# Sums of weight blocks: begun from SBUF, with GpSimd's queue doing the copies and additions in HBM

## The chip, the cores and the metric

The kernel runs on one core of a Trainium2 chip. Its time is the device time of one execution in microseconds (us). Before the change three runs took 359.33, 360.73 and 356.85 us, a median of 359.33. The profiled execution is one more run, of 360.87 us.

The engines are named as in the profile: PE multiplies matrices, PEld loads its weights, DVE is the vector engine, ACT the scalar engine, POOL is GpSimd, and SP only issues transfers. Each engine works through its own list of instructions in order. If one waits, everything behind it on that engine waits too. Transfers (DMAs) are issued here from SP's queue, and those that add to what is already at their destination from GpSimd's queue.

## The reference

Linear attention with product features, and behind it a block with a spatial gate. For every one of 4 batches:

```python
# attention, per head: phi(x) = outer product of S1 x and S2 x, flattened
kv  = einsum('bhsf,bhsd->bhfd', k_p, v);  z = sum(k_p, axis=2)
out = einsum('bhsf,bhfd->bhsd', q_p, kv) / (einsum('bhsf,bhf->bhs', q_p, z) + 1e-6)
# block: x is out with its heads side by side, (4, 1088, 128)
h = gelu(x @ w_in)                      # 1088 x 1024
u, v = h[..., :512], h[..., 512:]
v_n = (v - mean) / sqrt(var + 1e-6) * g_ln
v_s = einsum('ts,bsd->btd', w_sg, v_n) + b_sg    # the large product, 1088 x 1088
result = x + (u * v_s) @ w_out
```

The large product with `w_sg` is most of PE's work.

## The kernel before

All numbers are float32. A matrix is cut into a high and a low part (`w_h`, `w_l`, each of a form that PE multiplies fast), and a product takes three matmuls: high by high, low by high, high by low. `w_sg` transposed lies in SBUF as nine tiles of 128 rows by 1088 columns. The raw tiles are `w_f[0]` to `w_f[8]`. The pool that they lie in has ten buffers, so `w_l[0]` takes the tenth and `w_l[t]` the buffer of `w_f[t-1]` (`w_lo`, L806). `w_h` is cast on ACT (L798). The 1088 columns are cut in three (`CH`: 362, 362, 364).

From batch 1 on the kernel does not multiply with the first eight tiles and first two column blocks as they are. These make four quarters, and a scheme of the Strassen family (`pair`) uses seven products in place of eight. It needs four sums of quarters. `sums` makes them in HBM as `ud["1"]` to `ud["4"]`, each of 128 x 4 x 362 numbers (724 KB):

- `ud1` is the first four tiles' columns 0 plus their columns 1 (blocks of 362),
- `ud3` is columns 1 of the first four tiles plus columns 1 of the next four,
- `ud2` is `ud1` plus columns 1 of the next four,
- `ud4` is `ud2` plus columns 0 of the next four.

Before the change each sum begins with a copy within HBM on SP's queue (L1034), from the input or from an earlier sum, and then a DMA on GpSimd's queue adds the other quarter from the input to it (L1035).

`combine` brings each sum back in 16 steps (a sum's quarter of 181 KB each): a load into one of two `tmp` buffers (L1044), a cast to the high part on ACT (L1050), a subtraction for the low part on DVE (L1051), and two stores to `td` in HBM (L1052, L1053). The last four steps go straight to the tile `t4` in SBUF (L1046, L1047). It also stores the present block's parts (`td<-w_h` in one DMA, L1038, and `td<-w_l`, L1040). `stream` loads a sum's parts from `td` over a block of `w_h` and `w_l` just before the product that uses it (L1058, L1060).

`attention(b)` does the next batch's attention beside this batch's product. For each of three column pieces it loads q (`qld`, L1102), casts it on ACT (L1103), multiplies, stores the result to `dq` (L1114), and loads it back spread over partitions as `ea` (L1124) and `eb` (L1121). DVE multiplies these (L1127). Nine times it makes features of k: a small ACT copy `kb` (L1080), a DVE product `kp` (L335), two matmuls (L1085).

Batch 0 starts with a head (`Head`), whose order is a list of times (`HEAD`). What follows is ordered by `Plan`: every step is added with its engine, an assumed duration, what it reads and writes by key, and how long after its end others can use it (`late`). `order` then goes greedily: among the engines' next candidates it takes the step that can begin soonest, and among equals the one whose latest start is soonest. Each engine's clock begins at `START`. PE's own order comes from positions (`SIDE`, `UNITS`, `OUTS`). A key that no planned step has written counts as there from time 0: the planner does not know of the head's casts to `w_h`, so for it `td<-w_h` has no dependency. The planner decides only the order; on the chip real waits hold each engine.

The subtractions `w_l[t]` (L806, 1.29 in the planner) are steps of the plan. PE's low-half products of batch 0 (L1396) need them; the high-half ones (L1398, L1400) need only `w_h`. The subtraction for tile 8 also issues a memset on GpSimd (L805).

Of the kernel before, what the change touches and what calls it, by code (L numbers as in the profile page):

```python
# [9 lines left out]
F32 = mybir.dt.float32  # L10
# [4 lines left out]
ALU = mybir.AluOpType  # L15
# [19 lines left out]
START = dict(PE=51.0, V=50.5, A=49.5, G=42.0, SP=22.0)  # L35
# [3 lines left out]
        k=[-5.4506e+25, -1.86798e+26, -3.68831e+26, 1.20378e+26, -7.9147e+25, -9.67116e+25, 1.96766e+26, -2.06105e+26, 6.74955e+26],  # L39
        m=[7.0166e+17, 2.77359e+17, -3.64635e+17, 8.10316e+17, 1.97376e+17, -8.45712e+17, -4.46692e+17, -1.41243e+17, -1.88428e+17],  # L40
        q=[-9.85222e+37, 5.31737e+37, 4.53485e+37],
        n=[-274.09, -244.17, 66.1, 49.89, 93.41, 9.07],
        v=[76.03, 83.8, 72.28, 135.63, 69.13, 141.32, 90.81, 19.91, 17.47],
    ),
    dict(
        k=[593.03, 652.39, 759.38, 737.29, 443.29, 501.8, 757.29, 665.05, 583.46],
        m=[181.66, 55.3, 177.71, 207.99, 164.59, 28.04, 351.09, 71.24, 278.52],
        q=[311.71, 57.77, 475.27],
        n=[37.39, 79.03, 123.68, 46.32, 129, 236.43],
        v=[580.02, 111.55, 375.1, 240.14, 317.92, 200.21, 237.14, 270.19, 333.5],  # L50
    ),
    dict(
        k=[422.85, 473.07, 417.68, 478.31, 460.36, 386.01, 441.63, 346.1, 261.67],
        m=[301.77, 360.33, 343.21, 360.38, 350.42, 350.94, 332.88, 347.33, 369.39],
        q=[1146.3, 742.29, 1592.44],
        n=[984.53, 1257.57, 989.65, 894.74, 1102.64, 2169.93],
        v=[167.65, 154.05, 141.48, 171.91, 152.85, 155.69, 151.39, 163.95, 152.38],
# [3 lines left out]
    [-1.04603e+28, 1.31879e+27, 9.14156e+27],  # L61
    [3.41858e+18, 2.84867e+18, -6.26725e+18],
    [-189.15, -288.19, -100.37],
    [-50.81, 43.38, -20.02],
    [109.48, -67.17, 142.22],
    [148.1, -7.29, 2.09],
    [1056.04, 327.23, 85.89],
    [95.05, -21.61, 86.97],
    [117.32, 22.47, 794.73],
    [80.72, 480.77, 387.65],  # L70
    [-70.9, 427.98, 208.86],
    [-72.96, 32.18, 19.81],
    [1076.4, 485.65, 90.51],
    [2270, 600.47, 693.56],
    [395.39, -72.81, 275.88],
    [540.79, -121.68, 468.41],
]
OUTS = [
    [7.95, 65.22, 185.79],
    [-235.12, 49.59, -10.2],  # L80
    [30.85, -17.35, 3.84],
    [29.71, 41.29, 67.24],
    [211.45, -1.34, -11.66],
    [2.71, 252.59, 31.55],
    [237.53, 4.98, 393.45],
    [-7.96, 76.75, 88.15],
    [196.45, 360.61, 338.7],
    [19.67, 0.34, -44.95],
    [694.41, 120.49, 438.77],
    [26.72, 571.51, 1075.44],  # L90
    [202.88, 487.56, 87.11],
    [125.31, -0.94, 517.67],
    [304.16, 133.75, 3.31],
    [2.8, 474.19, 4.5],
# [161 lines left out]
def tile_kernel(ctx: ExitStack, tc: tile.TileContext, qd, kd, vd, sd, wd, bd, wind, gd, woutd, identd, outd):  # L256
    nc = tc.nc
    mm = nc.tensor.matmul
    V, A, G = nc.vector, nc.scalar, nc.gpsimd
    load = nc.sync.dma_start  # L260
# [41 lines left out]
    w_f, w_l = {}, {}  # L302
# [29 lines left out]
    def features(out, a, b):  # L332

        sh = [P, 2, R, 2, R]
        V.tensor_tensor(  # L335
            out.rearrange("t (p i h j) -> t p i h j", p=2, i=R, h=2),
            a[:, :32].rearrange("t (p i h) -> t p i h", p=2, i=R).unsqueeze(4).broadcast_to(sh),
            b.rearrange("t (p h j) -> t p h j", p=2, h=2).unsqueeze(2).broadcast_to(sh),
            op=ALU.mult,
        )  # L340
# [121 lines left out]
    class Head:  # L462
# [7 lines left out]
        def load(self, name, ns, f, after=()):  # L470
            self.s.at(name, "SP", 0.47, f, after, late=-ns)
# [377 lines left out]
    def load_(_, kb, f, **kw):  # L849
        return add("SP", 0.47, f, kb=kb, **kw)  # L850
# [10 lines left out]
    def ps(k):  # L861
        return pst[plan.got[k]]
# [20 lines left out]
    for t in range(NT):  # L883
        lo = add("V", 1.29, head.s.steps["wlo", t][2], w=[("w", t, c, 1) for c in range(3)], after=[lo] if t else [])
    done_lo = lo
# [138 lines left out]
    K2 = HW * 2  # L1024
# [3 lines left out]
    ud = {n: dram.tile([P, 4, K2], F32, name=f"ud{n}") for n in "1324"}  # L1028

    def sums():  # L1030
        part = lambda i, j: wd[:, 4 * i : 4 * i + 4, K2 * j : K2 * j + K2]
        for n, first, more in (("1", part(0, 0), part(0, 1)), ("2", "1", part(1, 1)), ("3", part(0, 1), part(1, 1)), ("4", "2", part(1, 0))):
            u = isinstance(first, str)
            load_("", 741, lambda n=n, f=first, u=u: load(ud[n], ud[f] if u else f), r=[("ud", first)] * u, w=[("ud", n)])  # L1034
            add("G", 1.2, lambda n=n, m=more: G.dma_start(ud[n], m, accum_op=ALU.add), w=[("ud", n)], late=7.0)  # L1035

    def combine():
# [25 lines left out]
    def attention(b):  # L1063
# [9 lines left out]
        for t in range(NT):  # L1073
# [7 lines left out]
            add("V", 0.38, lambda t=t, pk=pk: features(kpt[t % 3], ps(pk)[:, :P], kbt[t % 2]), r=[pk, ("kb", t % 2)], w=[("kp", t % 3)], free=[pk])  # L1081
# [297 lines left out]
    sums()  # L1379

# [95 lines left out]
```

## Time and profile before

| | |
|---|---|
| median of three runs | 359.33 us |
| profiled execution | 360.87 us |
| its span, first to last instruction | 359.1 us |
| mean granted TensorE clock | 0.976 |
| HBM read, written | 49.10 MB, 14.93 MB |
| DMA bytes on SP's queue, on GpSimd's | 55.05 MB, 2.97 MB |

In the timelines a row is: start and duration in us, engine, line, operation, what it writes and reads (buffer numbers left out), how many, and in brackets the idle time of the engine before it with what ended that. In a chain row there is only the start, the duration and the step; a chain's DMA row runs from issue to landing. In the rows of time stretches a pair is busy us and number of instructions for PE, PEld, DVE, ACT and POOL, and then come the granted clock of PE (1.00 is full), the mean busy share of the 16 DMA engines and GB/s. A DMA queue's row has packets, MB and the time of its packets as a share of 16 engines' time in the stretch. A row with "<-" and three numbers behind a colon is a wait: us in all, times, longest.

### The profile page before, as it was taken

Reading aid. Unit: us, or ns where it says so; the run is one execution under the profiler, and the core shown is the slowest. Engines: PE = TensorE matmul, PEld = TensorE weight load, DVE = VectorE, ACT = ScalarE, POOL = GpSimd, SP = SyncE. Lnnn points to the kernel's source line nnn. Section 1 sums busy time; section 2 is a strip of 40 time slices with the busy share of each in tenths; the row PEclk is TensorE's granted clock in tenths of the full one; section 3 lists DMA queues with packets and bytes.
Section 4 is the critical chain, followed back from the end, with each engine's and each line's share of the span. In section 5 each row is a group of like instructions: output and inputs, shape, how many; then the busy total and the mean of one; then the engine's idle time right before and its main releaser. Section 6 shows DMA issues by size and latency. Waiting matters only on the chain.

```text
span 359.1 us, 5751 instructions
## 1 busy us (share of the span) xinstructions
PE 338.1 (94%) x1952; PEld 316.2 (88%) x1952; DVE 260.0 (72%) x573; ACT 214.1 (60%) x509; POOL 28.4 (8%) x90
## 2 busy tenths in 40 slices
PE   8999999697499979999999999999999999999995
PEld 7867669696497979999999999998999999999994
DVE  4798999683766556989972688976885696674753
ACT  5476871360469977745679975657869552333421
POOL 0004001110000220000003300000041200000000
PEclk9999999899599998999999999999999999999999
DMA  7999997989357763595038506650005437002631
GB/s 251 394 374 299 174 228 166 236 271 204 114 150 241 219 195 92 164 340 157 21 102 259 150 15 191 185 192 4 2 0 168 165 112 242 0 23 60 181 112 62
DMA packets 41965, 58.47 MB, mean 163 GB/s; under 512 B 4080, under 2 KB 39216, under 8 KB 41904
## 3 DMA queue, kind: packets, MB, share of 16 engines
q1 hardware_dynamic: 39680, 55.05, 48.9%
q0 software_dynamic: 2112, 2.97, 6.2%
q8 instruction: 15, 0.25, 0.3%
q14 instruction: 14, 0.11, 0.1%
q10 hardware_dynamic: 144, 0.09, 0.1%
HBM read 49.10 MB, written 14.93 MB: 178 GB/s over the span
## 4 chain that ended last, share of the span: by engine, by line
PE 58%; DMA 16%; ACT 10%; DVE 8%; SPq 2%; issue 2%; POOL 1%; POOLq 0%; DVEq 0%; ACTq 0%
PE bz L992 10%; PE bz L994 10%; PE bz L993 10%; DMA eb<-dq 8%; DMA tmp<-ud 3%; DMA td<-tmp 3%; PE pz L792 3%; ACT vn L407 2%; PE pab L668 2%; ACT kp L1182 2%; DMA dq<-ab 2%; PE bs L1085 2%; ACT vn L1179 2%; PE bs L906 2%; PE bs L908 1%
## 5 line engine op out<-in xcount | busy, mean ns | idle before, releaser
L992 PE MATMUL bz<-w_h,ar 128*128 128x362 f32 (+1 forms) x288 | 97.3, 338 | 0.7 <-ACT ar L967 0.3
L994 PE MATMUL bz<-w_l,ar 128*128 128x362 f32 (+1 forms) x288 | 95.4, 331 | 0.0
L993 PE MATMUL bz<-w_h,ar 128*128 128x362 f32 (+1 forms) x288 | 95.4, 331 | 0.0
L992 PEld LDWEIGHTS bz<-w_h,ar 128*128 128x128 f32 x288 | 55.0, 191 | 2.9 <-DVE gt L922 1.7
L993 PEld LDWEIGHTS bz<-w_h,ar 128*128 128x128 f32 x288 | 55.0, 191 | 0.5
L994 PEld LDWEIGHTS bz<-w_l,ar 128*128 128x128 f32 x288 | 55.0, 191 | 0.0
L912 ACT ACTIVATE u<-bs 128x362 f32<-128x362 f32 (+1 forms) x48 | 22.6, 472 | 20.1 <-PE bs L908 13.6
L936 ACT CAST gh<-gt 128x362 fp32r<-128x362 f32 (+1 forms) x47 | 23.1, 493 | 16.7 <-DVE gt L935 9.7
L967 ACT CAST ar<-vn 128x512 fp32r<-128x512 f32 x37 | 22.8, 618 | 16.9 <-PE bz L994 15.9
L407 ACT ACTIVATE vn<-vn,st 128x512 f32<-128x512 f32 x36 | 27.5, 809 | 6.6 <-POOL st L538 2.6
L937 DVE TENSOR_TENSOR gl<-gt,gh 128x362 fp32r<-128x362 f32 (+1 forms) x47 | 24.8, 531 | 9.0 <-ACT gh L936 8.9
L935 DVE TENSOR_TENSOR gt<-gt,u 128x362 f32<-128x362 f32 (+1 forms) x47 | 24.8, 530 | 6.5 <-ACT u L912 6.1
L922 DVE SCALAR_TENSOR_TENSOR gt<-bz,g_col,b_bc 128x362 f32<-128x362 f32 (+1 forms) x37 | 21.9, 592 | 10.3 <-PE bz L1004 8.0
L968 DVE TENSOR_TENSOR ar<-vn,ar 128x512 fp32r<-128x512 f32 x37 | 25.3, 686 | 5.6 <-ACT ar L967 5.4
L906 PE MATMUL bs<-x_h,win_h 128*128 128x362 f32 (+1 forms) x48 | 17.0, 355 | 7.4 <-ACT u L912 7.4
L1127 DVE TENSOR_TENSOR ea<-ea,eb 128x728 f32<-128x728 f32 (+1 forms) x9 | 8.2, 914 | 20.2 <-DMA eb<-dq 20.2
L1182 ACT ACTIVATE kp<-vn,st 128x512 bf16<-128x512 f32 x27 | 19.4, 719 | 0.2
L1179 ACT ACTIVATE vn<-bs 128x512 f32<-128x512 f32 x27 | 16.0, 593 | 5.7 <-PE bs L1172 5.6
L1085 PE MATMUL bs<-vx,kp 128*128 128x128 f32 x108 | 16.5, 277 | 2.0 <-DVE kp L335 2.0
L792 PE MATMUL pz<-w_f,vn 128*128 128x362 f32 (+3 forms) x54 | 17.6, 472 | 0.5 <-ACT vn L407 0.5
L1085 PEld LDWEIGHTS bs<-vx,kp 128*128 128x128 f32 x108 | 14.8, 192 | 2.6 <-DVE kp L335 2.5
L906 PEld LDWEIGHTS bs<-x_h,win_h 128*128 128x128 f32 x48 | 9.4, 196 | 8.2 <-ACT u L912 7.7
(267 smaller groups left out, 757.0 us busy)
## 6 DMA issues: line engine op xcount, KB each, us to landing
w_l<-td SPq DMA_DIRECT2D x52, 181.0 KB
w_h<-td SPq DMA_DIRECT2D x26, 362.0 KB
w_f<-in_w SPq DMA_DIRECT2D x9, 544.0 KB
td<-tmp SPq DMA_DIRECT2D x24, 181.0 KB
ud<-in_w POOLq DMA_DIRECT2D x4, 724.0 KB, 11.5
tmp<-ud SPq DMA_DIRECT2D x16, 181.0 KB
vx<-in_v SPq DMA_DIRECT2D x8, 288.0 KB
ea<-dq SPq DMA_DIRECT2D x12, 182.0 KB
```

The source lines that it names most:

```text
L407: A.activation(self.vn(t), self.vn(t), AF.Identity, bias=self.nm[:, t : t + 1], scale=self.rs[:, t : t + 1])
L792: return mm(zs[ci], lhsT=vn[r, t, :P], rhs=w_f[t][r, c0 : c0 + cw], start=(t == 0), stop=(t == NT - 1),)
L906: mm(o, lhsT=win_h[:, ws], rhs=xh[:, cs], start=True, stop=False)
L935: add("V", dv(cw), lambda: V.tensor_mul(gt(k)[:, :cw], gt(k)[:, :cw], utt[plan.got[u]][:, :cw]), r=[u], w=[k], free=[u])
L937: add("V", dv(cw), lambda: V.tensor_sub(glt[plan.got[l]][:, :cw], gt(k)[:, :cw], f32(ght[plan.got[h]][:, :cw])), r=[h, k], take={l: "gl"}, ...
L968: add("V", dv(n), lambda: V.tensor_sub(dst[:, 1], q(), f32(dst[:, 0])), r=r, w=[key])
L992: mm(o, lhsT=ar[e][:, 0, t], rhs=wh, start=first, stop=False, skip_group_check=True)
L993: mm(o, lhsT=ar[e][:, 1, t], rhs=wh, start=False, stop=False, skip_group_check=True)
L994: mm(o, lhsT=ar[e][:, 0, t], rhs=wl, start=False, stop=last, skip_group_check=True)
L1085: mm(ps(pkv)[:, P * p : P * p + P], lhsT=kpt[t % 3][:, P * p : P * p + P], rhs=vx[:, NT : NT + t + 2 : t + 1] if p else vx[:, t : NT + 1 : ...
L1179: A.activation(g.vn(t), pair(ps(pv)), AF.Gelu_apprx_tanh, accum_out=g.mv[:, t, 0:1])
L1182: A.activation(pair(waste), g.vn(t), AF.Square, bias=g.mv[:, t, 0:1], scale=1.0, accum_out=g.mv[:, t, 1:2])
```

## The change

- `ud` is laid out as 4 tiles of 128 x 362, each tile in one piece.
- `ud1` and `ud3` begin with four stores each from the raw tiles in SBUF, on SP's queue, and four additions each from SBUF, on GpSimd's queue, 181 KB apiece.
- `ud2` and `ud4` begin with a copy within HBM that is now on GpSimd's queue, followed by the addition from the input as before.
- The raw tiles are now read by these transfers, so `w_l[t]` has to wait for the readers of `w_f[t-1]`. The steps for `w_l` are added to the plan behind `sums`, and the plan is told of this by the key `wf`; it assumes that the raw tiles are there at 31.0.
- `combine` takes the sums in the order 1, 3, 2, 4.
- The planner's numbers change: an addition of 181 KB is there 6 us after its issue, a copy 11, an addition of 724 KB 12 (7 before); `w_l` takes 1.2, `kp` 0.335; the clocks of GpSimd and SP begin at 34 and 24. The positions in `SIDE`, `UNITS` and `OUTS` are all new numbers.

```diff
-START = dict(PE=51.0, V=50.5, A=49.5, G=42.0, SP=22.0)
+START = dict(PE=51.0, V=50.5, A=49.5, G=34.0, SP=24.0)
...
     for t in range(NT):
-        lo = add("V", 1.29, head.s.steps["wlo", t][2], w=[("w", t, c, 1) for c in range(3)], after=[lo] if t else [])
-    done_lo = lo
+        add(None, 0, None, w=[("wf", t)], start=31.0)
...
-    ud = {n: dram.tile([P, 4, K2], F32, name=f"ud{n}") for n in "1324"}
+    ud = {n: dram.tile([4, P, K2], F32, name=f"ud{n}") for n in "1324"}
+
+    def plus(out, x, **kw):
+        add("G", 1.1, lambda: G.dma_start(out(), x, accum_op=ALU.add), late=6.0, **kw)
 
     def sums():
-        part = lambda i, j: wd[:, 4 * i : 4 * i + 4, K2 * j : K2 * j + K2]
-        for n, first, more in (("1", part(0, 0), part(0, 1)), ("2", "1", part(1, 1)), ("3", part(0, 1), part(1, 1)), ("4", "2", part(1, 0))):
-            u = isinstance(first, str)
-            load_("", 741, lambda n=n, f=first, u=u: load(ud[n], ud[f] if u else f), r=[("ud", first)] * u, w=[("ud", n)])
-            add("G", 1.2, lambda n=n, m=more: G.dma_start(ud[n], m, accum_op=ALU.add), w=[("ud", n)], late=7.0)
+        part = lambda t, j: w_f[t][:, K2 * j : K2 * j + K2]
+        for n, j, t1 in (("1", 0, 0), ("3", 1, 4)):
+            for t in range(4):
+                load_("", 186, lambda n=n, j=j, t=t: load(ud[n][t], part(t, j)), r=[("wf", t)], w=[("ud", n, t)])
+                plus(lambda n=n, t=t: ud[n][t], part(t + t1, 1), r=[("wf", t + t1)], w=[("ud", n, t)])
+        for n, m, j in (("2", "1", 1), ("4", "2", 0)):
+            k = [("ud", n, t) for t in range(4)]
+            add("G", 1.2, lambda n=n, m=m: G.dma_start(ud[n], ud[m]), late=11.0, r=[("ud", m, t) for t in range(4)], w=k)
+            add("G", 1.4, lambda n=n, j=j: G.dma_start(ud[n].rearrange(by), wd[:, 4:8, K2 * j : K2 * j + K2], accum_op=ALU.add), late=12.0, w=k)
...
-        for i, (n, t) in enumerate((n, t) for n in "1234" for t in range(4)):
+        for i, (n, t) in enumerate((n, t) for n in "1324" for t in range(4)):
...
-            load_("", 186, lambda n=n, t=t, x=x: load(x, ud[n][:, t]), r=[("ud", n)], w=[xk])
+            load_("", 186, lambda n=n, t=t, x=x: load(x, ud[n][t]), r=[("ud", n, t)], w=[xk])
...
-            add("V", 0.38, lambda t=t, pk=pk: features(kpt[t % 3], ps(pk)[:, :P], kbt[t % 2]), r=[pk, ("kb", t % 2)], w=[("kp", t % 3)], free=[pk])
+            add("V", 0.335, lambda t=t, pk=pk: features(kpt[t % 3], ps(pk)[:, :P], kbt[t % 2]), r=[pk, ("kb", t % 2)], w=[("kp", t % 3)], free=[pk])
...
     sums()
+    for t in range(NT):
+        k = [("w", t, c, 1) for c in range(3)]
+        lo = add("V", 1.2, head.s.steps["wlo", t][2], w=k + [("wf", t - 1)] * (t > 0), r=[("wf", t)], after=[lo] if t else [])
+    done_lo = lo
```

More of the change, by code (lines that the diff above doesn't have):

```diff
@@ L38 @@
     dict(
[L39 to L43, printed above, removed]
+        k=[-1.16361e+55, -3.98782e+55, -7.87392e+55, 2.56986e+55, -1.68965e+55, -2.06462e+55, 4.20061e+55, -4.39999e+55, 1.44091e+56],
+        m=[5.57221e+41, 2.20263e+41, -2.89574e+41, 6.4351e+41, 1.56746e+41, -6.7162e+41, -3.54739e+41, -1.12168e+41, -1.4964e+41],
+        q=[-2.17088e+69, 1.17165e+69, 9.99229e+68],
+        n=[-649.18, -1120.72, 1865.16, 28.1, -255, -4.66],
+        v=[73.84, 94.24, 75.32, 95.65, 110.33, 98.36, 69.74, 47.07, 100.34],
     ),
     dict(
[L46 to L50, printed above, removed]
+        k=[549.34, 540.97, 613.49, 599.12, 580.32, 517.97, 601.63, 551.67, 507.71],
+        m=[148.18, 41.04, 171.17, 28.14, 194.15, 14.31, 313.41, 62.96, 332.22],
+        q=[344.06, 72.79, 968.21],
+        n=[42.96, 404.73, 50.06, 42.49, 122.11, 266.46],
+        v=[477.02, 141.22, 300.65, 200.74, 258.56, 298.05, 141.09, 251.77, 155.94],
     ),
     dict(
[L53 to L57, printed above, removed]
+        k=[510.37, 556.72, 523.32, 512.01, 528.78, 475.68, 519.02, 521.04, 489.18],
+        m=[1352.97, 896.77, 1180.06, 1459.91, 620.33, 558.65, 842.81, 1057.47, 214.74],
+        q=[309.42, 2240.23, 1277.1],
+        n=[255.55, 1589.59, 408.99, 704.79, 560.06, 4045.78],
+        v=[255.16, 213.02, 143.76, 164.33, 160.55, 190.95, 180.49, 165.77, 196.42],
     ),
@@ L60 @@
 UNITS = [
[L61 to L76, printed above, removed]
+    [-5.01262e+63, 6.31962e+62, 4.38065e+63],
+    [7.34295e+47, 6.11878e+47, -1.34617e+48],
+    [-8.73177e+27, -7.3715e+27, 1.61033e+28],
+    [93.8, 46.52, 297.28],
+    [144, 31.57, 166.49],
+    [371.46, 6.26, -95.4],
+    [1936.81, 943.99, 649.03],
+    [522.53, 616.42, 585.81],
+    [274.07, 5.86, 906.65],
+    [-14.45, 244.49, 353.6],
+    [-27.54, 349.67, 340.18],
+    [-88.89, 31.34, 76.31],
+    [821.74, -29.95, 181.17],
+    [2178.52, 1311.75, 1297.67],
+    [241.81, -72.99, 531.16],
+    [582.02, 7.3, 580.69],
 ]
 OUTS = [
[L79 to L94, printed above, removed]
+    [-102.68, -5.72, 582.82],
+    [-711.17, -1.2, -346.35],
+    [-10.8, -16.42, 11.9],
+    [52.53, 0.23, 19.65],
+    [161.53, -11.48, 4.25],
+    [-17.57, 286.49, 347.85],
+    [370.36, 129.34, 484.21],
+    [-4.3, 75.9, 41.71],
+    [-44.37, 483.3, 456.97],
+    [36.4, 31.13, -46.65],
+    [393.4, 315.15, 10.02],
+    [44.56, 563.96, 1235.51],
+    [38.46, 555.94, 303.96],
+    [93.88, 8.07, 648.1],
+    [261.27, 337.04, 3.15],
+    [1.6, 431.95, 4.5],
 ]
```

## The prediction

> **What bounds the kernel now.** I read the page first, then what PE waited for, then the DVE, ACT, SP and POOL timelines at those places.
>
> ```profile
> span 359.1 us, 5751 instructions
> PE 338.1 (94%) x1952; PEld 316.2 (88%) x1952; DVE 260.0 (72%) x573; ACT 214.1 (60%) x509; POOL 28.4 (8%) x90
> ...
> 68.56 0.60 PE L1396 MATMUL bz<-w_l,ar 128*128 128x362 f32 x2 [3.03 <-DVE w_l L806]
> 94.51 0.67 PE L906 MATMUL bs<-x_h,win_h 128*128 128x362 f32 x1 [7.35 <-ACT u L912]
> 133.71 0.49 PE L1085 MATMUL bs<-vx,kp 128*128 128x128 f32 x2 [2.03 <-DVE kp L335]
> ...
> 69.80:73.10 3.30, 3.30 (x12) 3.30 (x12) 3.30 (x6) 1.88 (x5) 1.01 (x1) 0.50 1.19 333
> 94.60:100.40 5.80, 5.80 (x19) 5.80 (x20) 4.88 (x10) 2.78 (x7) 0.00 (x0) 0.50 0.65 199
> 134.70:138.00 3.30, 3.30 (x13) 3.30 (x12) 1.68 (x4) 1.66 (x4) 0.00 (x0) 0.50 0.39 108
> ```
>
> PE works 94% of the span, so the end is set by PE's order and its holes. Three are long: 3.03 + 7.35 + 2.03 = 12.4 us. Shortly after each of them the granted clock is 0.50 for a while (the number before the DMA share in the last three rows): 3.3 + 5.8 + 3.3 = 12.4 us at half speed, 6.2 us lost. Together 18.6 us: that is all this change could win if every hole went.
>
> What held PE there:
>
> ```profile
> 66.38 0.92 DVE L1127 TENSOR_TENSOR ea<-ea,eb 128x728 f32<-128x728 f32 x1 [4.20 <-DMA eb<-dq]
> 92.16 0.92 DVE L1127 TENSOR_TENSOR ea<-ea,eb 128x728 f32<-128x728 f32 x1 [8.35 <-DMA eb<-dq]
> ...
> 89.08 0.49 ACT L1103 CAST qth<-qld 128x364 fp32r<-128x364 f32 x1 [8.21 <-DMA qld<-in_q]
> 92.89 0.49 ACT L1050 CAST tmp<-tmp 128x362 fp32r<-128x362 f32 x1 [2.39 <-DMA tmp<-ud]
> ...
> 57.84 8.35 DMA eb<-dq
> 77.42 9.61 DMA td<-tmp
> 112.00 2.66 DMA td<-tmp
> 127.83 4.46 DMA eb<-dq
> ```
>
> The same transfers take 4.46 and 2.66 us late in the kernel, and 8.35 and 9.61 us in the chain ahead of the holes. What is beside them is GpSimd's additions into HBM:
>
> ```profile
> 33.16 1.48 POOL L1035 DMA_DIRECT2D ud<-in_w  x1
> 44.45 1.21 POOL L1035 DMA_DIRECT2D ud<-in_w  x1 [9.66 <-issue]
> 56.76 1.16 POOL L1035 DMA_DIRECT2D ud<-in_w  x1 [11.11 <-issue]
> 70.27 1.01 POOL L805 MEMSET w_l<- 64x1088 f32 x1 [12.35 <-DVE w_l L806]
> 77.23 1.19 POOL L1035 DMA_DIRECT2D ud<-in_w  x1 [5.96 <-DMA ud<-ud]
> ...
> DMA to landing us min/median/max: 10.8/11.5/13.6
> ...
> q0 software_dynamic: 526, 0.74, 78.4%
> q0 software_dynamic: 337, 0.49, 94.6%
> q1 hardware_dynamic: 92, 0.12, 14.1%
> ...
> DMA packets 742, 1.57 MB, mean 394 GB/s; under 512 B 46, under 2 KB 520, under 8 KB 741
> ```
>
> The q0 rows are GpSimd's queue, the first in 35 to 43 us, the second in 80 to 84 with SP's queue q1 below it; the last row is 24 to 28, where SP's queue is alone. An addition moves 0.74 MB in 8 us, or 0.49 MB in 4, and SP's queue gets 0.12 MB of those 4 us. So an addition (10.8 to 13.6 us) all but closes the DMA engines to others. The additions issued at 56.76 and 77.23 lie on the eb loads of the first two holes.
>
> **The change part by part.**
>
> *Sums 1 and 3 from SBUF.* Two HBM copies of 724 KB leave SP's queue during the head (the second is at 29.31 below); eight stores of 181 KB come in, and two additions of 724 KB become eight of 181. The head copies cost nothing now: in 30 to 36 us, the last row below, PE is busy 6.00 of 6.00 while the DMA share is 1.03. So I gain 0 from their going; were that cover gone, a copy would cost its 1.9 us. What matters is when the stores can go.
>
> ```profile
> 29.31 0.60 SPq L1034 DMA_DIRECT2D ud<-in_w  x1
> 41.30 0.39 SPq L1038 DMA_DIRECT2D td<-w_h  x1
> ...
> 49.93 0.48 SPq L1114 DMA_DIRECT2D dq<-ab  x1
> ...
> SPq L1038 <- ACT w_h L798: 11.3, 1, 11.3
> ...
> 30.00:36.00 6.00, 6.00 (x33) 4.52 (x32) 4.74 (x12) 3.23 (x6) 3.90 (x14) 1.00 1.03 301
> ```
>
> The planner takes, on each engine, what can begin soonest. It believes that the block `td<-w_h` (L1038) depends on nothing, and the stores on w_f from 31.0 on. So L1038 again stands ahead of the eight stores, and SP sits at it until ACT has cast w_h, 41.30 now. The stores therefore go at 41.7 to about 45.3 (eight at some 0.45), not at 31. The first lands after the 724 KB ahead of it: 724 KB at 394 GB/s is 1.9, a store like that at 112.00 is 2.66, so 41.7 + 4.6 = 46.3. The additions run from there, where now sum 1 has been going since 33.16. For one of 181 KB no row exists: it lies between a quarter of 10.8 (2.7) and the whole 11.5. I split 10.8 into 8 us of moving (0.74 MB in 35 to 43) and 2.8 of start and end, and take 2.8 + 1.5 to 2.0 per piece: the first lands at about 51, the fourth at 56, the eighth at 63.
>
> The Trainium skill (DMA: Bandwidth & Descriptors, Anatomy of one DMA) fits a GpSimd DMA as 2.0 us plus bytes over 436 GB/s, an estimate of 2.4 us for 181 KB. By it the first addition would land at 48.7 and this part would cost about 1 us, not 2.5. The trace disagrees for additions: the same fit gives 3.7 us for 724 KB, and 10.8 to 13.6 was measured.
>
> Who waits for that? In SP's order the loads of tmp 0 and 1 follow the stores (planned at 41 to 42), and behind them stand qld and dq, which feed the first eb load. On ACT, L1050 stands early:
>
> ```profile
> 49.88 0.51 ACT L1050 CAST tmp<-tmp 128x362 fp32r<-128x362 f32 x1
> 52.61 0.18 ACT L1080 COPY kb<-bs 128x32 f32<-128x32 f32 x1 [2.23 <-PE bs L1077]
> 52.69 0.50 ACT L1050 CAST tmp<-tmp 128x362 fp32r<-128x362 f32 x1
> ...
> 52.57 0.71 PE L1085 MATMUL bs<-vx,kp 128*128 128x128 f32 x4
> ...
> 71.11 1.28 DVE L806 TENSOR_TENSOR w_l<-w_f,w_h 64x1088 fp32r<-64x1088 f32 x1
> ```
>
> With tmp 0 landing at 51 + 2.66 = 53.7, ACT would stand from 49.88 for 3.8 us, with the kb copies behind it, and PE's L1085 behind those. PE has the high half of the second product to do meanwhile, where its order allows. dq is issued about 2.8 us later than 49.93, and the eb load then shares the engines with additions until 63 as it does now: DVE L1127 at 65 to 69 instead of 66.38. **I take +2.5 us** for this region; bounds 0 (all covered) and +8 (ACT's 3.8 in full, eb 2.6 late, 1.7 of half clock).
>
> *Write-after-read on w_f.* w_l[t] takes w_f[t-1]'s buffer, so it now waits for stores and additions that read it. The last w_l is made at 71.11 now; the eighth addition lands at about 63. Nothing, while this margin of 8 us holds. The memset of w_l[8] is on GpSimd's queue, in the plan between addition 2 (56.6) and copy 4 (70); it can't go before addition 2 is issued.
>
> *Copies and additions 2 and 4 on GpSimd's queue.* SP is rid of two issues of 0.52; on SP that is worth nothing beside its wait of 11.3. Copy 2, which SP issues early now, must stand behind the eight pieces: 63 + 1.9 + 2.66 = 67.6. Addition 2 then runs 67.6 to 79, copy 4 to 84 (as above) or 86 (it took 70.00 to 77.23 now), addition 4 from about 84 to 96 instead of 77.23 to 89.
>
> ```profile
> 70.00 0.52 SPq L1034 DMA_DIRECT2D ud<-ud  x1
> ...
> 79.80 0.33 SPq L1102 DMA_DIRECT2D qld<-in_q  x1
> 81.86 2.53 SPq L1121 DMA_DIRECT2D eb<-dq  x2
> ...
> 101.49 1.27 SPq L1121 DMA_DIRECT2D eb<-dq  x2
> ```
>
> This moves the collision of the second hole. Everything there is some 2.5 us late: qld at 82.3 lands before addition 4 starts, so ACT's 8.21 goes; eb is issued to 86.9 and lands between 84.4 + 4.46 = 88.9 (clear) and 96 (under the whole addition). I take 90.5, nearer to the clear end since an addition has a start of some 2 us. PE runs dry at 87.16 (94.51 - 7.35) + 2.5 and resumes 2.35 after DVE (94.51 against 92.16): a hole of 3.2 instead of 7.35. **-4.1 us**, and a half-clock window of 3.3 instead of 5.8, **-1.25**. Bounds: -7.35 - 2.9 and +1.
>
> Addition 4 now covers 84 to 96, where tmp and td go back and forth; td<-tmp may take 9.61 again. tmp has two buffers, so one late store need not stop the next load at once: **+1**, 0 to +3.5 (half of the 7 us by which 9.61 is over 2.66).
>
> *New planner numbers* (1.29 to 1.2, 0.38 to 0.335, landings of 6, 11, 12) change order only. Landings of 11 to 12 match the 11.5 measured, so tmp 8 to 15 are planned after their sums exist; this I count in the terms above.
>
> **Sum.** 2.5 - 4.1 - 1.25 + 1 = -1.85. The profiled execution took 360.87, its span and 1.8 around it, 1.5 above the median of 359.33; I apply the sum to the median: **357.5**, or 359.0 in a profiled execution like this one.
>
> **The rivals.**
> *Both holes go.* If the new order puts w_l ahead of L1127 and nothing of eb meets an addition, the 3.03, the 7.35 and their half clock (1.65 + 2.9) go, less 2.5 early: -12.4, 347. For it: the plan's landings are right now where 7.0 stood for 11.5. Against: the stores are late against the plan by over 10 us. 0.26.
>
> *GpSimd takes one addition at a time* (slower). Both waits of 9.66 and 11.11 carry no releaser but "issue", and end when the addition before has landed (33.16 + 10.8 = 43.96; 44.45 + 11.5). If pieces also wait for each other, eight take about 4.8 each: 46.3 + 38 = 84.7, w_l[8] is made at 86 instead of 71.11. PE stands 15 us, of which the holes of 3.03 and part of 7.35 are absorbed: +10, 369. It decides as soon as the eighth lands after 71. Against: what made those waits may be the size, and a piece is a quarter of it. 0.18.
>
> *The collision stays.* Eb lands at addition 4's end after all: 2.5 + 1 + 1 - 0 = +4, 363. 0.10.
>
> *Copies on few DMA engines.* If a copy of 724 KB whose outermost dimension is 4 ran on 4 of 16 engines, 394 GB/s becomes 98: 7.4 us instead of 1.9 twice, so addition 4 moves on by 11, to 95 to 107, onto the eb load of 101.49. That adds a stall of about 2 and a half-clock window, 361. 0.06. The Trainium skill (DMA: Bandwidth & Descriptors, Why a DMA increments its semaphore by 16 and not by 1) states that the engines used are the largest number up to 16 that divides the slowest dimension of both patterns; by it the rival holds if the shape is carried as [4, 128, 362]. No run here shows it yet.
>
> **Chances.** About 1% is what a measurement of this kernel can tell from no change. My forecast has 0.40: 357.5, its own range 352 to 363 from the bounds; of it 0.13 is faster than 355.7, 0.23 within, 0.04 slower than 362.9. Adding the rivals (347 faster; 369 slower; 363 half within, half slower; 361 within): faster 0.39, same 0.34, slower 0.27. The range of 8 in 10 reaches 345 to 369.
>
> **What would show it.** Right: SP's wait at L1038 stands, stores after 41; the first L1035-like addition after 45; ACT waits at L1050 near 50; addition 4 issued at 80 to 88; the hole near 90 is under 4. Wrong: stores at 31 (then everything is 10 us earlier and the first rival is likelier); waits "issue" of 3 to 5 between small additions; PE waiting for w_l after 72.

## The result, and the profile after

The changed kernel takes 370.75 us (median of 4 runs, 368.27 to 373.07) against 358.67 us for the kernel before beside it (4 runs, 356.85 to 360.73). The ratio is **1.033, with a 95% interval of 1.024 to 1.043**: slower by 3.3%. The prediction was 357.5 us with a range of 345 to 369, so both its sign and its range missed. The profiled executions, 369.28 against 360.87 us, hold 8.4 of the 12.1 us; the trace explains those. The times given here and below are medians of all runs, and the ratios leave out the slow ones, so the two can differ by a few tenths of a per cent.

First the page of the kernel after: the sums of its busy times, and the line for GpSimd's queue.

```profile
span 367.4 us, 5790 instructions
PE 338.0 (92%) x1952; PEld 316.9 (86%) x1952; DVE 261.3 (71%) x573; ACT 216.8 (59%) x509; POOL 33.1 (9%) x98
...
q0 software_dynamic: 2272, 4.45, 7.2%
```

PE has the same work as before, 338.0 us against 338.1. The span is 8.3 us longer, so the time went into holes. GpSimd's queue now moves 4.45 MB instead of 2.97: the two copies of 0.74 MB came over to it.

Next, the PE rows of the timeline of after that begin after a long wait, in the same form as in the prediction:

```profile
64.94 0.80 PE L1083 MATMUL bs<-sk,vn 128*128 128x128 f32 x2 [10.78 <-ACT ab L1119]
78.55 1.22 PE L1091 MATMUL bs<-vx,kp 128*128 128x128 f32 x4 [2.46 <-DVE kp L335]
99.83 0.67 PE L945 MATMUL po<-gl,wout_h 128*128 128x362 f32 x1 [5.17 <-DVE gl L936]
```

Two of the holes of before are still there and smaller: 3.03 became 2.46, and 7.35 became 5.17. The first row is new: PE stands 10.78 us from 54.16 to 64.94, where before it had no long hole. With two shorter ones of 1.55 and 1.57 us near 121 and 138, the holes over 1.5 us add up to 21.5 us where they were 12.4. That is 9.1 more for a span that grew by 8.3. The time at half clock grew, but not the work in it: in the first stretch below, 10.2 us at a granted clock of 0.50, PE was busy for only 3.06 us, and for 5.67 in the second. With a third of 3.4 us around 80 that is some 12 us of work, as before.

```profile
57.80:68.00 10.20, 3.06 (x12) 3.07 (x13) 3.49 (x5) 3.26 (x12) 1.86 (x2) 0.50 0.97 217
98.80:105.50 6.70, 5.67 (x19) 5.67 (x20) 6.31 (x15) 4.35 (x9) 0.00 (x0) 0.50 0.54 158
```

What led to the new hole is a chain over four engines. Here are SP's waits between 40 and 66 us in after (us in all, times, longest):

```profile
SPq L1044 <- ACT w_h L798: 15.5, 1, 15.5
SPq L1050 <- DMA ud<-w_f: 8.2, 2, 7.5
```

And the timelines of after, first SP, then GpSimd, ACT and DVE:

```profile
42.47 0.38 SPq L1044 DMA_DIRECT2D td<-w_h  x1
42.90 5.32 SPq L1036 DMA_DIRECT2D ud<-w_f  x8
55.83 1.35 SPq L1050 DMA_DIRECT2D tmp<-ud  x2
...
48.17 6.58 POOL L1030 DMA_DIRECT2D ud<-w_f  x7 [14.45 <-DMA ud<-w_f]
56.07 0.88 POOL L1030 DMA_DIRECT2D ud<-w_f  x1 [1.32 <-issue]
60.00 0.56 POOL L1040 DMA_DIRECT2D ud<-ud  x1 [2.93 <-DMA ud<-w_f]
...
61.57 0.49 ACT L1056 CAST tmp<-tmp 128x362 fp32r<-128x362 f32 x1 [11.91 <-DMA tmp<-ud]
62.71 0.49 ACT L1056 CAST tmp<-tmp 128x362 fp32r<-128x362 f32 x1 [0.65 <-DMA tmp<-ud]
63.11 1.13 ACT L966 CAST ar<-vn 128x512 fp32r<-128x512 f32 x2
64.15 0.18 ACT L1086 COPY kb<-bs 128x32 f32<-128x32 f32 x1
...
64.43 0.45 ACT L1119 COPY ab<-bs 64x364 f32<-64x364 f32 x1
...
64.36 0.42 DVE L335 TENSOR_TENSOR kp<-bs,kb 128x256 f32<-128x256 f32 x1 [11.29 <-ACT kb L1086]
```

SP stands 15.5 us at the block `td<-w_h`, until ACT has cast `w_h`. Only then do the eight stores go, at 42.90. The first has landed when GpSimd begins to add at 48.17. The first sum is there when SP's load of `tmp` goes, at 55.83. ACT reached its cast of `tmp` at 49.66 and stands there 11.91 us. Behind it on ACT stand the casts to `ar`, the first copy `kb` and the copy `ab`; DVE stands 11.29 for that `kb`; and PE, which has done everything else by 54.16, stands until `ab` is copied.

Rows of the chain of waits of after give the transfers in the middle (the second small addition and the second load of `tmp`, which landed last), and last a load ahead of the hole of 5.17:

```profile
42.90 4.65 DMA ud<-w_f
49.01 7.84 DMA ud<-w_f
56.87 5.83 DMA tmp<-ud
...
84.65 9.61 DMA ea<-dq
```

### The profile page after: what moved, and what is told of

The parts are those of the page before. It is cut to its first block, busy times and chain, and to the rows that moved or that the text cites. A ratio compares the mean times of both kernels' runs of the same rounds, so it can differ in the third digit from the quotient of the medians.

```text
span 367.4 us, 5790 instructions
## 1 busy us (share of the span) xinstructions
PE 338.0 (92%) x1952; PEld 316.9 (86%) x1952; DVE 261.3 (71%) x573; ACT 216.8 (59%) x509; POOL 33.1 (9%) x98
## 3 DMA queue, kind: packets, MB, share of 16 engines
q1 hardware_dynamic: 39712, 53.56, 47.5%
q0 software_dynamic: 2272, 4.45, 7.2%
## 4 chain that ended last, share of the span: by engine, by line
PE 56%; DMA 21%; DVE 11%; ACT 6%; SPq 2%; issue 2%; POOL 1%; DVEq 0%; POOLq 0%
PE bz L991 10%; PE bz L993 10%; PE bz L992 10%; DMA eb<-dq 7%; DMA td<-tmp 5%; DMA tmp<-ud 3%; DMA ud<-w_f 3%; DMA ea<-dq 3%; PE po L945 2%; PE pab L668 2%; PE po L943 2%; PE po L944 2%; PE bs L905 2%; PE bs L907 2%; PE bs L906 2%
## 5 line engine op out<-in xcount | busy, mean ns | idle before, releaser
L991 PE MATMUL bz<-w_h,ar 128*128 128x362 f32 (+1 forms) x288 | 96.1, 334 | 0.4 <-DVE gt L921 0.4
L992 PE MATMUL bz<-w_h,ar 128*128 128x362 f32 (+1 forms) x288 | 94.5, 328 | 0.0
L993 PE MATMUL bz<-w_l,ar 128*128 128x362 f32 (+1 forms) x288 | 94.4, 328 | 0.0
L991 PEld LDWEIGHTS bz<-w_h,ar 128*128 128x128 f32 x288 | 54.3, 189 | 2.0 <-DVE gt L921 0.9
L992 PEld LDWEIGHTS bz<-w_h,ar 128*128 128x128 f32 x288 | 54.2, 188 | 0.6
L993 PEld LDWEIGHTS bz<-w_l,ar 128*128 128x128 f32 x288 | 54.1, 188 | 0.0
L966 ACT CAST ar<-vn 128x512 fp32r<-128x512 f32 x37 | 22.7, 618 | 23.9 <-PE bz L993 23.8
L921 DVE SCALAR_TENSOR_TENSOR gt<-bz,g_col,b_bc 128x362 f32<-128x362 f32 (+1 forms) x37 | 21.5, 587 | 7.8 <-PE bz L1003 6.6
L335 DVE TENSOR_TENSOR kp<-bs,kb 128x256 f32<-128x256 f32 x27 | 11.2, 420 | 17.9 <-ACT kb L1086 17.4
L1083 PE MATMUL bs<-sk,vn 128*128 128x128 f32 x54 | 11.3, 293 | 12.4 <-ACT ab L1119 10.8
L1083 PEld LDWEIGHTS bs<-sk,vn 128*128 128x128 f32 x54 | 9.6, 199 | 13.5 <-ACT ab L1119 11.1
L945 PE MATMUL po<-gl,wout_h 128*128 128x362 f32 (+1 forms) x47 | 16.2, 345 | 5.2 <-DVE gl L936 5.2
L1091 PEld LDWEIGHTS bs<-vx,kp 128*128 128x128 f32 x108 | 15.5, 202 | 4.6 <-DVE kp L335 4.6
```

Of the source, the lines that this page charges most:

```text
L945: mm(o, lhsT=wout_h[:, db], rhs=hl, start=False, stop=i == NB, skip_group_check=True)
L966: add("A", ac(n), lambda: A.copy(dst[:, 0], q()), r=r, w=[key])
L991: mm(o, lhsT=ar[e][:, 0, t], rhs=wh, start=first, stop=False, skip_group_check=True)
L992: mm(o, lhsT=ar[e][:, 1, t], rhs=wh, start=False, stop=False, skip_group_check=True)
L993: mm(o, lhsT=ar[e][:, 0, t], rhs=wl, start=False, stop=last, skip_group_check=True)
L1091: mm(ps(pkv)[:, P * p : P * p + P], lhsT=kpt[t % 3][:, P * p : P * p + P], rhs=vx[:, NT : NT + t + 2 : t + 1] if p else vx[:, t : NT + 1 : ...
```

## The experiments

Where a kernel below moves a step, the planner's list is made as in the changed kernel, and then one step is put behind another; no other step leaves its place in the list, though ACT's order, into which the head's steps are merged, can shift (by one place in the first kernel, by more where it is said). Each ratio is to the kernel before, run again beside that kernel (medians 357.85 to 358.88 us). The added lines move line numbers up by some (L1044 of after is L1052 in the first one).

### The block behind the stores

```diff
+        seq = self.order(free, t0)
+        # behind(i, j): take step i out of seq and put it behind step j
+        behind(mark["block"], <the last of the eight stores>)
```

> Only the store of the block td<-w_h moves on SP's list, from ahead of the eight stores of w_f to behind them; all other orders stay. Theory (SP held the sums): the stores go at about 28 to 32 us instead of 42.9, the first small addition at about 34 instead of 48.2, ACT no longer waits 11.9 us for tmp, and PE's hole of 10.78 us goes with its half-clock time: 357 to 359 us; if the hole of 5.17 near 97 goes as well, because the last addition then ends near 80 instead of 93, 351 to 354. Rival (the small additions from SBUF are slow in themselves): tmp still lands after 55, a hole of 5 us or more stays, 364 or more. Rival (the new order is bad elsewhere): the hole goes and others come, 366 or more.

Measured: 359.85 us, ratio 1.005 (1.003 to 1.008). So 10.9 of the 12.1 us lost go when one issue on SP's queue changes its place. SP, ACT and PE in its timeline:

```profile
26.68 6.49 SPq L1044 DMA_DIRECT2D ud<-w_f  x8
42.23 0.37 SPq L1052 DMA_DIRECT2D td<-w_h  x1
42.70 1.21 SPq L1058 DMA_DIRECT2D tmp<-ud  x2
...
52.98 0.50 ACT L1064 CAST tmp<-tmp 128x362 fp32r<-128x362 f32 x1 [4.33 <-DMA tmp<-ud]
...
56.12 0.49 PE L1091 MATMUL bs<-sk,vn 128*128 128x128 f32 x2 [2.20 <-ACT ab L1127]
```

And a row of its chain of waits:

```profile
42.70 10.26 DMA tmp<-ud
```

The stores go 16 us earlier and the hole near 55 falls from 10.78 to 2.20. But the load of `tmp`, issued right behind the block, takes 10.26 us, and ACT still waits 4.33. The kernel is no faster than before: its long holes (2.20, 0.98, 3.27, 2.59, 1.61 and 0.99 us) sum to 11.6, hardly less than the 12.4 of before, where the prediction's picture of the later holes would have left 8.3 (3.03, 3.2 and 2.03).

### Only ACT's casts later

The block stays where the change put it. The first two casts of `tmp` go behind the third `kb` on ACT, and the stores that need them behind the first `eb` loads on SP.

```diff
+        for i in (1, 0):
+            behind(mark["cast", i], mark["kb", 1, 2])
+        for i in (1, 0):
+            behind(mark["high", i], mark["fill", 1, 0, 1])
```

> The block stays ahead of the stores; on ACT the casts of the first two tmp tiles go behind the third kb copy, and on SP their two stores to td behind the first eb loads. Theory (what costs is ACT standing at a load that the held stores make late, with the kb copies behind it): PE's hole of 10.78 shrinks to 4 or less although the sums are as late as before; the first dq is issued near 57.5 instead of 65.4; 361 to 364 us. Rival (the late sums cost by themselves, through w_l or the DMA engines): the time stays at 368 or more.

Measured: 368.61 us, ratio 1.029 (1.024 to 1.035), 2 us under the changed kernel, a difference that the intervals do not tell from nothing (that of the changed kernel is 1.024 to 1.043). The time is the rival's. The hole of 10.78 shrinks to 6.37, and the two others grow: 2.46 becomes 4.72, and 5.17 becomes 5.67 (at 94.5). The first two, from PE in its timeline, and the first moved cast on ACT:

```profile
63.57 0.80 PE L1094 MATMUL bs<-sk,vn 128*128 128x128 f32 x2 [6.37 <-DVE kp L345]
77.21 1.22 PE L1102 MATMUL bs<-vx,kp 128*128 128x128 f32 x4 [4.72 <-DVE kp L345]
...
59.27 0.49 ACT L1067 CAST tmp<-tmp 128x362 fp32r<-128x362 f32 x1 [5.48 <-DMA tmp<-ud]
```

And one of SP's waits in this kernel:

```profile
SPq L1141 <- DMA dq<-ab: 8.1, 1, 8.1
```

`dq` is issued at 55.5 instead of 65.4, but then needs over 8 us to land among the late additions. And ACT still stands at the moved cast, 5.48 us, now with the later `kb` copies behind it. So this kernel shortens the stand on ACT and does not remove it; what late sums cost with ACT free, it does not show.

### The old planner numbers, and the old numbers with the block moved

The first kernel has the change's new data path with `START`, `SIDE`, `UNITS` and `OUTS` of before. The second one adds to it that the block goes behind the first `eb` loads.

```diff
-START = dict(PE=51.0, V=50.5, A=49.5, G=34.0, SP=24.0)
+START = dict(PE=51.0, V=50.5, A=49.5, G=42.0, SP=22.0)
...
+        behind(mark["block"], mark["fill", 1, 0, 1])   # the second kernel only
```

> The changed data path with the planner's numbers of before (START, SIDE, UNITS, OUTS), so a third order. In it GpSimd's clock begins at 42, so the planner expects the first tmp some 8 us later and puts the casts behind the first kb copies. Theory (the loss is one of order): the hole near 55 is under 5 and the time 358 to 364. Rival (the stores and small additions cost by themselves): 368 or more.

> The planner's numbers of before with the changed data path, and the block td<-w_h behind the first eb loads. With the block in its place this order took 371.6. Theory (the block's place is the cause whatever the order): the hole of 7.55 near 58 goes, 355 to 360 us. Rival (the old numbers don't suit the new path): 364 or more.

Measured: 371.61 us, ratio 1.038 (1.033 to 1.043), for the first; 364.48, ratio 1.018 (1.013 to 1.023), for the second. The new positions are therefore not what cost the time: with the old ones the loss is the same, SP again stands 16.0 us at the block, and PE has a hole of 7.55 near 60. Expecting these numbers to give back part of the loss was wrong. With the block moved that hole is gone and 7 us come back, but holes of 3.66 and 5.99 us come at 65 and 70, the second behind a `qld` load of 10.65 us that was issued at 64.11, just behind the block at 63.01. 364.48 is what the rival said.

### GpSimd's additions as plain copies

All ten DMAs of GpSimd that add become copies of the same bytes, so the sums are left out. Nothing else is changed; then the same with the block behind the stores.

```diff
-G.dma_start(out(), x, accum_op=ALU.add)
+G.dma_start(out(), x)
...
-..., wd[:, 4:8, K2 * j : K2 * j + K2], accum_op=ALU.add)
+..., wd[:, 4:8, K2 * j : K2 * j + K2])
```

> GpSimd's ten additions become plain copies of the same bytes from the same places, so the sums are left out; every order stays. If adding is what closes the DMA engines: the addition that was 7.84 us in the chain takes about 4, a GpSimd transfer of 724 KB lands in 5 to 6 instead of 10 to 12, the hole of 10.78 shrinks to about 6 and that of 5.17 to under 3, 362 to 365 us. If GpSimd's queue is slow whatever it does: as with the additions, 369 or more.

> The block right behind the eight stores, as in the first run, and GpSimd's ten additions as plain copies of the same bytes (the sums are left out: each destination holds only the last quarter copied into it). It asks whether adding costs by itself. With the block ahead of the stores, plain copies gained 7.8 us (370.75 to 362.99). Theory (adding slows every transfer beside it, wherever it stands): the gain stays most of that against the 359.9 of the same order with additions: 352 to 355, a ratio of 0.982 to 0.990. Rival (the adding cost only through the late first sum, since the hold on SP multiplied it): the gain shrinks to 0 to 3 us, 357 to 360.

Measured: 362.99 us, ratio 1.014 (1.008 to 1.019), with the block ahead; 354.01, ratio 0.988 (0.983 to 0.993), with the block behind the stores. Both times are the theory's, though the holes with the block ahead are 8.44 and 3.84 us, where about 6 and under 3 were expected. Against the same orders with additions (370.75 and 359.85) the adding costs 7.8 and 5.8 us. So it is not a cost of the late first sum alone; most of it is there in an order without the hold. The issue-to-landing times of all twelve DMAs that GpSimd issues into `ud` (the ten, and in both kernels the two copies for `ud2` and `ud4`), first with the block behind the stores and additions, then in the same order with copies:

```profile
DMA to landing us min/median/max: 4.1/7.6/11.0
```

```profile
DMA to landing us min/median/max: 3.6/4.8/7.8
```

The copies also leave the hold in place when the block stays ahead. In the chain of waits of that kernel (block ahead, plain copies):

```profile
47.20 6.35 DMA ud<-w_f
53.57 5.84 DMA tmp<-ud
```

And ACT in its timeline:

```profile
59.43 0.89 ACT L1056 CAST tmp<-tmp 128x362 fp32r<-128x362 f32 x2 [10.31 <-DMA tmp<-ud]
```

ACT's 11.91 only becomes 10.31. The stall is a matter of when the stores go, and of how full the DMA engines are at that moment: the `tmp` load takes 5.84 with no addition anywhere.

### The block far behind, alone and with the casts

```diff
+        behind(mark["block"], mark["fill", 1, 0, 1])
```

The second kernel also has the two casts and two stores of the experiment above.

> Only the block moves, behind the first eb loads. Beside it the list of ACT changes at one place: the first tmp cast slips in ahead of four head steps near 43 us. Theory: tmp 0 lands at 44 to 46, so the head's four steps wait 1 to 3 us there; the second cast doesn't wait; the hole near 55 is under 2; 355 to 359 us. Rival (tmp loads take 10 us with the additions alone beside them): ACT waits there 5 us or more, 362 or more.

> Both cures together: the block td<-w_h goes on SP's list behind the first eb loads, the first two tmp casts on ACT behind the third kb copy, their stores behind the first eb loads. Theory (the late sums made ACT and SP stand, and what stayed with the block right behind the stores was the tmp load of 10.3 us beside it): the first additions start near 35, tmp lands by 48, ACT doesn't wait at the casts, PE has no hole over 1 us before 60; the first dq is issued near 51 instead of 65.4; 352 to 356 us. Rival (the additions on the DMA engines cost PE wherever they lie): holes of 3 us or more come elsewhere and the time stays at 358 to 361.

Measured: 361.62 us, ratio 1.010 (1.004 to 1.016), and 361.63, ratio 1.007 (1.002 to 1.011). Neither theory has the time. With the block alone moved, the first cast slips ahead of four steps of the head, ACT waits 3.50 us at it, and PE has holes of 2.88 at 43.8 and 3.00 at 67.0. With both there is no long hole before 60, and `dq` goes at 52.84. What comes in its place, from the chain of waits of the kernel with both:

```profile
62.36 7.97 DMA qld<-in_q
72.97 7.35 DMA qld<-in_q
```

And ACT in its timeline:

```profile
70.36 0.49 ACT L1121 CAST qth<-qld 128x360 fp32r<-128x360 f32 x1 [9.25 <-DMA qld<-in_q]
```

The block at 60.13 and copy 4 at 60.72 now lie on the first of these loads, and addition 4 at 69.28 on the second. PE has holes of 3.25, 4.30 and 3.05 between 63 and 82.

### The block behind the first two loads of tmp

```diff
+        behind(mark["block"], <the later of the loads of tmp 0 and 1>)
```

> On SP's queue the block td<-w_h stands behind the eight stores and behind the loads of tmp 0 and 1; all else is the changed kernel's order. In the run with the block right behind the stores both tmp loads were issued at 42.70, behind the block, and landed at 52.98, so that ACT still stood 4.33 us at the cast. Theory (whose bytes are ahead on the engines decides): tmp 0 is issued as soon as the first addition has landed, 40 to 43, lands by 47, ACT waits under 1 us there, and the time is 1 to 3 us under that run's 359.9: 357 to 359, a ratio of 0.995 to 1.000 to the kernel before. Rival (the block's 741 KB only change their victim): ACT does not wait at the cast, but qld, dq or the first eb load land some 4 us later, and the time is 359.5 to 362.

Measured: 358.45 us beside 357.85, ratio 1.004 (1.001 to 1.007). In its chain of waits are the first small addition and the first load of `tmp`:

```profile
35.08 4.65 DMA ud<-w_f
39.75 5.91 DMA tmp<-ud
```

ACT did not wait at a cast near 50, but it waited 2.90 at 45.68: the cast had come ahead of the last `vn` steps of the head in ACT's order, and PE lost 2.28 there. Then `qld` was waited for again, 4.19, and a hole of 3.05 followed at 67.4. Of the two texts the theory has the time right (its ratio is just above the one given) and the wait wrong, and the rival has the new victims right. With the change's own numbers, the place of the block, once it is behind the stores, is worth nothing that can be measured here.

### Planned anew with what the traces show

The planner learns that the block's parts are there at 42, the raw tiles at 27, and that a transfer of GpSimd is there for GpSimd's own next step only after its landing time; then the order is made anew.

```diff
-        return self.OWN.get(a["eng"], 0) if a["eng"] == b["eng"] and a["eng"] != "SP" else a["late"]
+        return self.OWN.get(a["eng"], 0) if a["eng"] == b["eng"] and a["eng"] != "SP" and a["late"] < 6.0 else a["late"]
...
-        add(None, 0, None, w=[("wf", t)], start=31.0)
+        add(None, 0, None, w=[("wf", t)], start=27.0)
+    for t in range(4, 8):
+        add(None, 0, None, w=[("w", t, 1, 0)], start=42.0)
```

> The changed kernel with three of the planner's numbers put right: the block td<-w_h is told of the casts (there at 42), the raw tiles are there at 27, and a transfer on GpSimd's queue is ready for the next one there only after its landing time. The rest of the order is made anew. Theory (the planner's view of the block made the loss): the stores go first, no hole over 4 us, 354 to 360. Rival (the greedy order with these positions is bad for other reasons): 364 or more.

Measured: 359.81 us, ratio 1.000 (0.996 to 1.005). The loss is gone, and nothing is gained: long holes of 1.92, 2.69, 3.08, 1.84 and 1.69 us stand for the three of before.

### The sums on GpSimd itself, in SBUF

If adding by DMA is what costs, it can be left to the engine: GpSimd adds tile by tile into the four parts of `tmp` (`sl` below), and SP stores each sum to `ud`. No DMA adds any more. The planner has the numbers of the last experiment, but the block's parts at 60, and the order is made anew.

```diff
+        for t in range(4):
+            b, d, c = part(t, 1), part(t + 4, 1), part(t + 4, 0)
+            wk = [("wf", t), ("wf", t + 4)]
+            for k, n, x, y, r in ((0, "1", part(t, 0), b, []), (1, "3", b, d, []), (2, "2", sl[0], d, [sk[0]]), (3, "4", sl[2], c, [sk[2]])):
+                add("G", 0.8, lambda k=k, x=x, y=y: G.tensor_add(sl[k], x, y), r=wk + r, w=[sk[k]])
+                load_("", 186, lambda k=k, n=n, t=t: load(ud[n][t], sl[k]), r=[sk[k]], w=[("ud", n, t)])
```

> No DMA adds at all: GpSimd itself makes the four sums, tile by tile, from the raw tiles in SBUF into the four parts of tmp (16 additions of 128x362), and SP stores each to ud (16 stores of 181 KB); copies 2 and 4, the eight additions from SBUF and the two of 724 KB go. The planner takes 0.8 us for an addition and places the block td<-w_h at 60. Theory (what is left to win is the DMA work of adding, as the run with the block last and plain copies gave 354.0 against 359.9): no transfer is slowed by an addition, the holes near 68 and 90 fall below 3 us, and the time is 351 to 356, a ratio of 0.98 to 0.995. Rival (the stores of the sums now wait on SP for GpSimd, up to about 50, and qld and dq behind them are late): a hole of 3 us or more near 60 to 70, and the time is 358 to 364.

Measured: 361.96 us beside 358.02, ratio 1.012 (1.007 to 1.018). The time is the rival's, but its hole near 60 to 70 is not there; the middle of the kernel is as the theory had it, with no hole above 1.74 us between 50 and 100. Here is the stretch of 50 to 100 us, first of the kernel before, then of after, then of this one (PE's busy time comes first, the granted clock third from the end):

```profile
50.00:100.00 50.00, 39.59 (x222) 37.72 (x221) 35.36 (x65) 16.51 (x41) 3.35 (x3) 0.87 0.79 198
```

```profile
50.00:100.00 50.00, 31.19 (x174) 28.54 (x173) 27.26 (x46) 15.18 (x41) 10.37 (x13) 0.85 0.99 217
```

```profile
50.00:100.00 50.00, 47.16 (x267) 41.54 (x267) 44.61 (x84) 30.43 (x76) 1.00 (x1) 1.00 0.59 178
```

PE is busy 47.16 of 50 us at full clock, 7.6 more than before. But it is 3.7 us behind in the stretch 30 to 50 (15.81 busy against 19.49) and 5.1 in 145 to 160 (9.76 against 14.85). The first of these two shows on DVE, in the head. The same three instructions, first in the kernel with the block behind the stores, then here:

```profile
35.20 0.69 DVE L498 SCALAR_TENSOR_TENSOR wi0t<-win_raw,wi0t 128x512 int32<-128x512 int32 x1
35.80 0.42 DVE L500 TENSOR_SCALAR wi0m<-win_raw 128x512 int32<-128x512 int32 x1
37.58 1.27 DVE L813 TENSOR_TENSOR w_l<-w_f,w_h 128x1088 fp32r<-128x1088 f32 x1
```

```profile
36.25 1.31 DVE L491 SCALAR_TENSOR_TENSOR wi0t<-win_raw,wi0t 128x512 int32<-128x512 int32 x1
37.49 1.17 DVE L493 TENSOR_SCALAR wi0m<-win_raw 128x512 int32<-128x512 int32 x1
40.91 1.91 DVE L806 TENSOR_TENSOR w_l<-w_f,w_h 128x1088 fp32r<-128x1088 f32 x1
...
35.90 2.47 POOL L1039 TENSOR_TENSOR tmp<-tmp,w_f 128x362 f32<-128x362 f32 x2
```

Beside GpSimd's additions (the last row) each of them takes 0.6 to 0.75 us longer, and DVE is what the head's last steps wait for. The loss at 145 to 160 is a hole of 3.83 at 146.7. It ends with ACT's cast to `ar`, which waited 2.38 us for a `tmp` that DVE (L1227) made at 149.13; whether another order would avoid it was not tried. So this time does not show what it is worth by itself that no DMA adds.

## Why the prediction was wrong

**Step by step.** SP standing at the block: right, 15.5 us, stores from 42.90 (41.7 predicted). First store landed: about 47.5 (46.3). Additions: the first sum was there at 55.83 (51), the fourth at 60.0 (56). `tmp` 0 landed at 61.5 (53.7). ACT standing at the cast: right in kind, 11.91 us instead of 3.8. Copy 2 went at 60.00 (63 to 65 by its landing of 67.6), addition 2 at 65.45 (67.6), copy 4 at 75.05 (79), addition 4 at 82.50 (84). GpSimd's part was right to 5 us at every step, with errors both ways: the first sums came 4 to 5 us later and copy 2 some 3 to 5 earlier, since it stood behind the fourth small addition and not behind the eighth.

**The step that failed is the "+2.5" for the stores that come late.** Its mechanism was seen and its size was not: that region cost a hole of 10.78 us, more than the upper bound of 8. The 7.8 us by which `tmp` 0 came later than worked out are three errors in one direction: 1.2 for the store, 3.6 for the first addition (8.3 from its store's landing, where 4.7 were taken), and 3.0 for the load (5.7, where the quiet row of 2.66 was taken). The prediction had itself shown rows of 8.35 and 9.61 for small transfers beside additions, and used them for the holes of before; for the transfers that the change puts beside eight stores, eight additions and the block it took quiet prices. In after the two queues take turns. From 48 to 51 us only SP's queue has packets (the first row below: packets, MB and share of the engines' time), though GpSimd issues additions from 48.17 on; from 52 to 56 only GpSimd's has (the second row):

```profile
q1 hardware_dynamic: 484, 0.62, 109.4%
q0 software_dynamic: 480, 0.62, 136.9%
```

So the first addition's bytes moved only when those of the stores were nearly through, and then beside those of the seven behind it: it took 7.6 us from its issue. In the kernel with the block behind the loads of `tmp`, where 0.28 MB of stores were left at its issue and not 0.7, it took 4.65 (the row at 35.08 above), the 4.7 that the prediction took. The load of `tmp` met the later additions: from 56 to 60 SP's queue moved 0.13 MB and GpSimd's 0.59.

**The second half of the same error is who stands behind the cast.** The prediction put "the kb copies behind it", and the high half of the second product on PE as cover. Both were true: PE's cover lasted from 49.66 to 54.16, and 4.5 us were hidden. But the cast had come to the head of ACT's list, also ahead of the copy `ab` for which PE's next instruction stood (L1119 at 64.43) and of the casts to `ar` that it needs soon after (L966 at 63.11), so once the cover was used up nothing was left. In the plan the latest start of this cast is 45.8, before ACT's own beginning at 49.5, because the chain from it to the product that needs the sum is long; among steps that can begin at the same time the earliest latest start goes first.

**The second hole, "-4.1".** 7.35 became 5.17, not 3.2: half of the gain. Addition 4 was issued at 82.50 and `ea` at 84.65, which took 9.61 (the last row of the chain above). The prediction's text had this as the unfavourable end, "under the whole addition", and took a value nearer to the other end. `eb` was issued only at 90.01 to 92.38 (86.9), and DVE could multiply at 97.97, even later than that end of 96. That the hole was no longer is luck: PE too ran dry later, at 94.66 and not at 89.66. The half clock there stayed as it was, 5.67 us of work against 5.80, where -1.25 was counted. The "+1" for `tmp` and `td` beside addition 4 can't be told from this.

**Write-after-read on the raw tiles, "nothing".** Right in cost, wrong in its picture. The memset of the last `w_l` was not between addition 2 and copy 4 but behind addition 4, at 85.67: the planner counts only 0.1 us between two steps of GpSimd, so its plan has the last addition issued at 47.0, and the new landing times of 11 and 12 never applied inside that chain. It cost nothing only because DVE, itself late, came to the last tile at 85.80.

**The rivals.** *One addition at a time* is refuted: seven were issued in 6.58 us without a wait, and the eighth waited 1.32. *Copies on few engines* too: in the trace a copy is 16 packets of 46,336 bytes, a sixteenth of it each and all under way at once, and the first was there 5.4 us after its issue (60.00 to 65.45), beside other traffic. *Both holes go* was wrong, and *the collision stays* was half right, at 5.17 (its sum, 2.5 + 1 + 1, is 4.5 and not 4). None of them had the slower end for its real cause: the place of one issue on SP's queue. That 369, the figure of *one addition at a time*, lies so near to 370.75 is chance. The slower rival should have been the one that the prediction held in its hands, ACT at the cast with everything crowded.

**What the runs show as cause.** Shown: moving the block behind the stores brings back all but 0.5% (five orders of the change's own numbers with it out of the way lie at 1.000 to 1.010), and the loss is there with the planner's old positions too. Not shown is how much of it ACT's place in the chain makes by itself: moving its casts gave 2 us, within the noise. Shown too: adding by DMA costs 5.8 us even with the block out of the way. That beginning the sums in SBUF therefore had little to win, since as many bytes are added by DMA as before, in ten pieces instead of four, is an argument; no run took the pieces apart. Open is where the 3.7 us lie by which the medians differ more than the two profiled executions. No version beat the kernel before with its full computation; the best equalled it.

## What to carry to other kernels

A transfer that waits on a queue holds everything behind it, so before costing a new early transfer, look at what stands ahead of it on its queue and when that is really released; the place of one issue was worth 11 us here. Price a transfer by rows from the crowd that it will stand in, not by the quietest row of the same size. And when a stall appears on an engine, read its list from there to the instruction that feeds the busiest engine: the length of the cover decides what the stall costs (here 4.5 us of 11.91 were covered).

## What the runs showed of the hardware that was not expected

- DMAs that add landed later here than plain copies. With the same bytes, places and order, GpSimd's twelve transfers into `ud` landed in a median of 7.6 us when ten of them added and of 4.8 when none did, and the kernel took 359.85 against 354.01 us. With the block ahead, additions moved 0.62 MB in the 4 us from 52 to 56, and plain copies 1.03 MB in the 4 us from 51 to 55.
- A small transfer pays for what is ahead of it, on its own queue and on the other. The `tmp` load of 181 KB took 10.26 us right behind the block of 741 KB, and 5.91 with the block behind it; a store of that size took 2.66 in a quiet place (`td<-tmp` at 112.00 of before). In the first of these, additions had the engines until 46 us (0.69 MB in 42 to 46, SP's queue 0.07), and then SP's queue, with the block ahead of the load (0.90 MB in 46 to 50). The Trainium skill (DMA: Bandwidth & Descriptors, Queues, rings and completion order) states that each DMA engine takes the descriptors of a queue in ring order. The rows agree with that as far as the block is concerned; until 46 it was the other queue that had the engines.
- GpSimd's elementwise work slows some of DVE's instructions: 0.42 us became 1.17, 0.69 became 1.31, 1.27 became 1.91; DVE's statistics (L770, BATCH_NORM_STATS2), also beside additions at 43.56, took 0.66 as in the other kernel. The Trainium skill (SBUF — State Buffer, SBUF: two separate sides) states that the two engines share a pair of ports, which a GpSimd instruction, or a DVE instruction of certain kinds, holds to its end while the other waits. The rows agree: each of the three is longer by 0.62 to 0.75 us, less than the 0.83 to 1.89 us of one addition in that stretch.
